# Recalling a compressive memory in transposed layout: one matmul per unit, denominators in a column-tiled pass, reciprocals broadcast by DMA, and projections that begin on two chunks of x

## The chip, the cores and the metric

The kernel runs on one core of a Trainium2 chip. The metric is device time in microseconds (us) of one execution.

Engines are named as in the profile: PE (matmuls; PEld is its weight loads), DVE (the vector engine), ACT (the scalar engine), POOL (GpSimd), SP (the sync engine, which here only issues DMAs; "SPq" in a listing). "L473" is a line of that kernel's own source, so the numbers differ between kernels. A line of a helper (`matmuls`, here L468 or L473) stands for many tiles.

## The reference, cut to what matters

```python
# x: (1, 2048, 512); 32 heads of 16; 4 segments of 512 tokens
g = sigmoid((x * gate_w).sum(-1, keepdims=True))          # one gate per token
for s in range(4):                                        # M, z: memory of the earlier segments
    p = softmax(qs @ ks.T * scale + causal_mask)
    a_dot = p @ vs
    a_mem = (phi(qs) @ M) / ((phi(qs) @ z) + 1e-6)        # the recall, per head
    o = sig(beta) * a_mem + (1 - sig(beta)) * a_dot
    M += phi(ks).T @ vs;  z += phi(ks).sum(tokens)
a = o @ wo
b = ((relu(x @ W_gate)) * (x @ W_up)) @ W_down            # the FFN, F = 1792
return g * a + (1 - g) * b
```

The kernel computes (1 - g) * (r * a + b) with the ratio r = g / (1 - g) = exp(z), so r, one number per token, must reach the attention's outputs.

## The kernel before

A unit is one chunk of 128 channels (eight heads) of one segment; there are 16 units, and 12 of them (segments 1 to 3) recall the memory. A small list scheduler inside the kernel (`plan.add(engine, duration, key, emit, dependencies, latency)`) fixes the order of instructions on every engine before the program is built. A table `SHIFT` of offsets to the keys holds the tuning. Each engine gets its own list in that order and works it in order.

The recall of a unit, with `normalise` shared with the attention itself:

```python
    def recall(seg, c):
        for r in range(2):                                  # even heads, odd heads
            a = plan.add("PE", 216, key + r, lambda r=r, sl=sl: nc.tensor.matmul(
                bank(sl), lhsT=mbd[i][:, c, r].rearrange("p j e -> p (j e)"), rhs=pqT[u % RQ][:],
                start=True, stop=True), ...)
            groups.append((sl, a))
        recalled[u] = normalise(u, 1, key, groups)          # m = 1

    def normalise(u, m, key, groups):
        for r, (sl, a) in enumerate(groups):                # two 128x512 transposes on DVE
            done.append(plan.add("DVE", 633, ..., nc.vector.transpose(T[ts.i][:, r], bank(sl)) ...
        if m: ...  den = den + 1e-6                          # column DH of T
        ...  cfr = reciprocal(den)
        ...  cfr = cfr * grc[i][:, c, m]                     # head gate times r
        ...  och = T[..., 0:DH] * cfr                        # 128x512
    # ... cut
```

The ratio r reaches `grc` through DRAM, from the 128x4 tile `rcol` (token 128t+p in partition p, column t):

```python
            def back():
                for j in range(4):
                    nc.sync.dma_start(out=rq[seg % 2][32 * j:32 * j + 32],
                                      in_=ratio[seg].rearrange("b q t -> q b t"))
            d = plan.add("SP", 360, key, lambda: nc.sync.dma_start(
                out=ratio[seg].rearrange("b q t -> (b q) t"), in_=rcol[:, cols]), [c], 1700)
            d = plan.add("SP", 1440, key, back, [d, ...], 1700)
```

At the start, 10 warm-up matmuls run, then 16 transposes of x (four per chunk), then the projections, each of which needs all four chunks.

The softmax here doesn't subtract the row's maximum and nothing guards it: scores larger than these inputs give would overflow.

Of the kernel before, what the change touches and what calls it, by code (L numbers as in the profile page):

```python
# [7 lines left out]
BF16 = mybir.dt.bfloat16  # L8
F32 = mybir.dt.float32
# [18 lines left out]
RE = 7  # L28
# [4 lines left out]
    21: -90000, 25: -170000, 29: -240000, 31: 210000, 52: 30000, 55: -10000, 58: -140000,  # L33
    74: 40000, 81: 90000, 85: 33000, 87: 80000, 88: -40000, 94: -80000, 115: 80000, 121: 100000,
    145: 130000, 204: -20000, 207: -50000, 210: -20000, 213: -3000, 222: -20000, 227: 270000,
    231: 1500, 234: 15600, 237: 30000, 240: -120000, 243: 11999, 246: 2000, 249: -10000,
    252: -14000, 255: 12999, 261: 28000, 264: -2000, 267: 30000, 270: 15000, 273: 28000,
    276: -10000, 279: 20000, 282: -2000, 300: -120000, 312: 24999, 324: -80000, 339: 80000,
    351: -50000, 354: 60000, 364: -20000, 372: -20000, 377: -50000, 379: 70000, 380: -40000,
    383: -100000, 385: 20000, 398: 10000, 400: 100000, 401: 10000, 404: 16000, 406: -130000,  # L40
    407: -4000, 480: -200000, 481: -190000, 544: 50000, 553: -18000, 556: 6000, 559: -30000,
    562: 2000, 565: -10000, 574: 19000, 583: -20000, 586: -10000, 589: -30000, 592: 9000,
    595: 10000, 598: 27000, 604: 2000, 607: -10000, 610: -4000, 613: -3000, 619: -10000,
    628: 21000, 631: -10000, 637: 29999, 661: 69999, 673: 70000, 686: 180000, 687: 150000,
    688: 100000, 689: -100000, 701: -120000, 704: 140000, 705: 110000, 709: -280000, 714: 15000,
    722: -6000, 727: -60000, 735: 15000, 737: 150000, 748: 8000, 751: -90000, 754: -60000,
    757: -10000, 796: -180000, 800: 90000, 801: 10000, 830: -160000, 831: -20000, 834: 140000,
    869: 30000, 903: 5000, 906: 40000, 909: -3000, 915: -15000, 921: -20000, 924: -10000,
    927: 10000, 930: 30000, 933: 10000, 936: 30000, 942: 30000, 945: -30000, 951: -10000,
    957: -20000, 963: -30000, 969: -20000, 972: 30000, 978: 40000, 984: 24000, 987: 209999,  # L50
    999: 110000, 1011: 60000, 1037: -230000, 1038: 60000, 1039: -260000, 1042: -100000,
    1046: -60000, 1047: 50000, 1052: -40000, 1054: -90000, 1057: 30000, 1062: -80000,
    1067: 56000, 1072: -60000, 1077: -50000, 1082: -70000, 1090: 50000, 1093: -20000,
    1096: 20000, 1134: -30000, 1170: 40000, 1239: 14000, 1242: 90000, 1247: 119999, 1248: 99999,
    1251: 10000, 1254: 60000, 1257: -20000, 1263: -2000, 1266: 20000, 1272: 50000, 1275: 60000,
    1278: 140000, 1284: 50000, 1290: 20000, 1293: -70000, 1296: -30000, 1299: -30000,
    1323: 159999,
# [157 lines left out]
def kernel(  # L215
# [34 lines left out]
    xn = [sb([P, 4, D], BF16, f"xn{i}") for i in range(2)]  # L250
# [17 lines left out]
    mbd = [sb([P, NC, 2, 4, 32], BF16, f"mbd{i}") for i in range(2)]  # L268
    mzacc = sb([P, NC, 2, HW], F32, "mzacc")
    hT = ring([P, L], BF16, "hT", RH)  # L270
    T = ring([P, 2, L], F32, "T", 2)
# [4 lines left out]
    och = ring([P, L], BF16, "och", 4)  # L276
    cfr = ring([P, 2, 16], F32, "cfr", 4)
# [7 lines left out]
    def work():  # L285
# [3 lines left out]
    LANDS = dict(n0=4500, q=5950, k=9300, v=9750, g0=11800, u0=13300, gw=13900, g1=15200, u1=16700,  # L289
                 x1=18400, g2=20400, u2=21600, g3=22800, u3=24000, d0=27700, d1=30400, o=31800, n1=33400,  # L290
                 x2=35200)
# [11 lines left out]
    def load_halves(dst, src, k, name):  # L303
        src = src.rearrange("(c p) n -> p c n", p=P)
        nc.sync.dma_start(out=dst[:, 0:k // 2], in_=src[:, 0:k // 2])
        nc.scalar.dma_start(out=dst[:, k // 2:k], in_=src[:, k // 2:k])
        return arrival(name)
# [4 lines left out]
    def load_xn(seg):  # L312
        nc.sync.dma_start(out=xn[seg % 2][:], in_=x[seg * L:(seg + 1) * L, :].rearrange(
            "(t p) n -> p t n", p=P))
# [12 lines left out]
    got_n[0] = load_halves(xn[0], x[0:L, :], 4, "n0")  # L327
# [9 lines left out]
    got_x[1] = [arrival("x1")]  # L337
# [6 lines left out]
    load_xn(1)  # L344
    got_n[1] = arrival("n1")
    load_xT(2)
    got_x[2] = [arrival("x2")]
    plan.add("SP", 33100, -1e9, None)
# [9 lines left out]
    for j in range(4):  # L358
        nc.vector.memset(mcol_e[32 * j:32 * j + 16, :], 1.0)
    nc.vector.tensor_scalar(mcol_o[:], mcol_e[:], -1.0, 1.0, ALU.mult, ALU.add)  # L360
    bd = sb([P, NC, 8, HW], BF16, "bd")
    nc.gpsimd.memset(bd[:], 1.0)
    nc.gpsimd.affine_select(out=bd[:], in_=bd[:], compare_op=ALU.is_ge, fill=0.0, base=0,
                            pattern=[[0, NC], [-16, 8], [0, HW]], channel_multiplier=1)
    nc.gpsimd.affine_select(out=bd[:], in_=bd[:], compare_op=ALU.is_ge, fill=0.0, base=15,
                            pattern=[[0, NC], [16, 8], [0, HW]], channel_multiplier=-1)
    for i in range(2):
        nc.gpsimd.memset(Vp[i][:, :, :, DH:18], 1.0)
        nc.vector.memset(mbd[i][:], 0.0)
# [13 lines left out]
    gcat = sb([P, NC, 2, 2], F32, "gcat")  # L383
    grc = [sb([P, NC, 2, 2, 16], F32, f"grc{i}") for i in range(2)]
# [4 lines left out]
    ratio = [dram.tile([4, 32, 4], F32, name=f"ratio{i}") for i in range(NSEG)]  # L389
    rq = [sb([P, 4, 4], F32, f"rq{i}") for i in range(2)]  # L390

    def head_gates():
        gb = gcat[:, :, 1, :]
        for j in range(4):
            nc.vector.tensor_copy(ebq[32 * j:32 * j + 32], eb.rearrange(
                "p (c j r) -> p j c r", j=4, r=2)[32 * j:32 * j + 32, j])
        nc.vector.tensor_scalar(gb, ebq[:], 1.0, None, ALU.add)
        nc.vector.reciprocal(gb, gb)
        nc.vector.tensor_tensor(gcat[:, :, 0, :], ebq[:], gb, ALU.mult)
# [3 lines left out]
    got_gates = plan.add("DVE", 1250, 0.0, head_gates, [got_eb], 100, lock=True)  # L403
# [11 lines left out]
    def gate_tasks(seg):  # L415
# [3 lines left out]
        for t in range(4):  # L419
            zs.append(plan.add("DVE", 690, key, lambda t=t: nc.vector.scalar_tensor_tensor(  # L420
                junk[:], xn[seg % 2][:, t, :], 1.0, gwb[:], ALU.mult, ALU.mult,
                accum_out=zc[:, 4 * seg + t:4 * seg + t + 1]), [got_n[seg], got_gw], 60, lock=True))
# [20 lines left out]
        else:  # L443
            src, frees = lambda: rq[seg % 2].rearrange("p b t -> p t b"), []

            def back():
                for j in range(4):
                    nc.sync.dma_start(out=rq[seg % 2][32 * j:32 * j + 32],
                                      in_=ratio[seg].rearrange("b q t -> q b t"))
            d = plan.add("SP", 360, key, lambda: nc.sync.dma_start(  # L450
                out=ratio[seg].rearrange("b q t -> (b q) t"), in_=rcol[:, cols]), [c], 1700)
            d = plan.add("SP", 1440, key, back, [d, att.get(("gate", seg - 2))], 1700)
        war = [att.get(("comb", 4 * seg - 5))]
        att["gate", seg] = plan.add("DVE", 500 if seg else 340, key, lambda: nc.vector.tensor_tensor(
            grc[seg % 2].rearrange("p c m r (t b) -> p (c m r) t b", b=4),
            src()[:, None].to_broadcast([P, 16, 4, 4]),
            gcat.rearrange("p c m r -> p (c m r)")[:, :, None, None].to_broadcast([P, 16, 4, 4]),
# [4 lines left out]
    def matmuls(key, deps, sl, ops, start=True, stop=True, prev=None, width=L, need=()):  # L462
        n = len(ops)
        for k in range(0, n, GM):
# [7 lines left out]
            t = plan.add("PE", 215.8 * width / L * m, key - (0 if first else CONT), emit, deps,  # L472
# [6 lines left out]
    def x0_tasks():  # L479
        done = []  # L480
        for c in range(NC):
            sl = work()

            def pe(c=c, sl=sl):
                tp = bank(sl).bitcast(BF16)
                for t in range(4):
                    nc.tensor.transpose(tp[:, t * P:(t + 1) * P], xn[0][:, t, c * P:(c + 1) * P],
                                        ident[:])
            a = plan.add("PE", 240, K(-9), pe, [got_n[0]], PEL, need=[sl])
            cp = nc.scalar.copy if c % 2 else nc.vector.tensor_copy  # L490
            done.append(plan.add(
                "ACT" if c % 2 else "DVE", 430, K(-9), lambda c=c, sl=sl, cp=cp: cp(  # L492
                    xT[0][:, c, :], bank(sl).bitcast(BF16)[:, 0:L]),
                [a], DVL, frees=[sl]))
        return done
# [14 lines left out]
    def proj_q(seg, c):  # L510
# [4 lines left out]
        a = matmuls(key, got_x[seg] + [got_q] + war, sl, proj_mm(wq_sb, c, seg))  # L515
# [9 lines left out]
    def proj_k(seg, c):  # L525
# [3 lines left out]
        a = matmuls(key, got_x[seg] + [got_k] + war, sl, proj_mm(wk_sb, c, seg))  # L529
# [53 lines left out]
    def attention(seg, c):  # L583
# [47 lines left out]
        a, oc = normalise(u, 0, key, groups)  # L631
        if seg:
            b, om = recalled[u]
            a = plan.add("DVE", 335, key, lambda: nc.vector.tensor_tensor(
                och[oc.i][:], och[oc.i][:], och[om.i][:], ALU.add), [a, b], 110, frees=[om],
                lock=True)
        war = [ffn.get(("o", seg - 2, q)) for q in range(4)]
        att["ot", u] = plan.add("DVE", 633, key, lambda: nc.vector.transpose(
            oT[i][:, c, :], och[oc.i][:]), [a] + war, DVL, frees=[oc])

    recalled = {}

    def normalise(u, m, key, groups):
# [15 lines left out]
        a = done[1]  # L659

        def den():
            return t()[:, :, :, DH]
        if m:
            a = plan.add("DVE", 150, key, lambda: nc.vector.tensor_scalar(
                den(), den(), 1e-6, None, ALU.add), [a], 40, lock=True)
# [176 lines left out]
```

## Time and profile before

| | before |
|---|---|
| time | 278.38 us median of 3 runs (277.8 to 278.51) |
| span of the profiled run | 276.3 us |
| busy: PE / DVE / ACT / POOL | 265.3 / 207.7 / 195.9 / 87.5 us |
| first projection, last matmul (starts) | 7.39, 272.9 us |

Part 1 of the profile's page for the kernel before (busy us, share of the span, instructions):

```profile
PE 265.3 (96%) x2178; PEld 113.1 (41%) x2214; DVE 207.7 (75%) x456; ACT 195.9 (71%) x176; POOL 87.5 (32%) x139
```

PE is the limit, and the span is nearly full of it. Ends of matmuls are modelled, so this share says little about the last few per cent. The rest of this text therefore uses starts: "lag" is what PE has lost, from its first projection up to some matmul, against its own list worked without a wait (0.2158 us per 512 columns, about 0.1 us at each change of the tiling mode, as between 71.93 and 72.03 us; both from the timeline of the kernel before). By that count the kernel before is 7.39 us of start + 260.09 us of PE work + 5.41 us of lag = 272.9 us, the start of the last matmul.

The view of waits, PE's (line, waited for: us in total, times, longest), shows how little is lost to any one cause:

```profile
PE ps L468 <- issue: 1.9, 12, 0.2
PE ps L779 <- DVE mcol_e L357: 1.3, 1, 1.3
PE ps L578 <- ACT E L598: 0.7, 2, 0.4
PE ps L468 <- DVE T L651: 0.6, 2, 0.4
```

The view of windows (start:end, length, then busy us of PE, PEld, DVE, ACT, POOL with the number of instructions, PE's granted clock, DMA share, GB/s) for two stretches:

```profile
60.00:65.00 5.00, 4.75 (x44) 2.04 (x38) 4.56 (x13) 3.30 (x4) 0.64 (x1) 1.00 0.01 3
...
90.00:99.30 9.30, 9.14 (x60) 3.71 (x61) 7.29 (x18) 7.02 (x4) 3.46 (x5) 1.00 0.08 17
```

PE is busy 4.75 of 5 and 9.14 of 9.3 us there, at full clock.

### The profile page before, as it was taken

How to read it: one execution, taken by the hardware profiler on the slowest of the kernel's cores; microseconds unless marked ns; L12 is line 12 of the kernel's file. 1: busy time of each engine (PE TensorE's matmuls, PEld its weight loads, DVE VectorE, ACT ScalarE, POOL GpSimd, SP SyncE). 2: the span in 40 equal slices, each digit the busy share in tenths (PEclk: the TensorE clock that was granted, in tenths of full speed). 3: DMA queues.
4: the chain of work that ended last, by engine and by line, in shares of the span. 5: the costliest groups of instructions: out<-in, count | busy, mean ns of one | idle time of the engine just before them, and what ended most of it. 6: DMA issues, size and time to landing. Idle time of an engine off the chain costs nothing.

```text
span 276.3 us, 5510 instructions
## 1 busy us (share of the span) xinstructions
PE 265.3 (96%) x2178; PEld 113.1 (41%) x2214; DVE 207.7 (75%) x456; ACT 195.9 (71%) x176; POOL 87.5 (32%) x139
## 2 busy tenths in 40 slices
PE   8899999989999999999999999999999999999995
PEld 4343444433343433434343434343444334344543
DVE  3688989999898869698998768999228785638322
ACT  2299898968897778899996878778847776734100
POOL 5013333432424343534334343333301435230000
PEclk9999999999999999999999999999999999999999
DMA  7999965100411100100001000000000000000001
GB/s 233 316 269 347 268 93 171 13 14 0 97 22 20 23 19 21 21 0 19 4 0 36 7 19 5 19 19 2 0 0 4 19 21 19 21 0 0 2 28 48
DMA packets 27993, 15.46 MB, mean 56 GB/s; under 512 B 15680, under 2 KB 27968, under 8 KB 27968
## 3 DMA queue, kind: packets, MB, share of 16 engines
q1 hardware_dynamic: 26752, 14.06, 19.4%
q10 hardware_dynamic: 1216, 1.06, 1.1%
q8 instruction: 17, 0.28, 0.4%
q14 instruction: 8, 0.07, 0.1%
HBM read 9.86 MB, written 2.10 MB: 43 GB/s over the span
## 4 chain that ended last, share of the span: by engine, by line
PE 81%; DVE 10%; ACT 4%; issue 4%; DVEq 0%; ACTq 0%
PE ps L468 63%; PE ps L578 8%; PE ps L620 6%; PE ps L681 2%; ACT E L598 2%; PE ps L779 2%; DVE hT L743 1%; ACT ex L507 1%; DVE ktr L532 1%; DVE T L651 1%; DVE junk L420 1%; DVE QT L517 1%; ACT rgr L737 1%; DVE och L656 1%; ACT Vp L561 0%
## 5 line engine op out<-in xcount | busy, mean ns | idle before, releaser
L598 ACT ACTIVATE E<-ps 128x2048 bf16<-128x2048 f32 x80 | 150.6, 1882 | 31.5 <-PE ps L578 26.8
L607 POOL TENSOR_SCALAR_AFFINE_SELECT E<-E 128x512 bf16<-128x512 bf16 x128 | 83.9, 671 | 157.5 <-ACT E L598 157.5
L743 DVE TENSOR_TENSOR hT<-ps,rgr 128x512 bf16<-128x512 f32 x56 | 38.2, 685 | 29.3 <-PE ps L468 21.4
L468 PE MATMUL ps<-xT,wg_sb 128*128 128x512 bf16 x214 | 56.9, 379 | 1.3 <-issue 0.3
L468 PE MATMUL ps<-xT,wu_sb 128*128 128x512 bf16 x220 | 55.8, 380 | 0.8 <-issue 0.5
L468 PE MATMUL ps<-wd_sb,hT 128*128 128x512 bf16 (+1 forms) x233 | 54.5, 367 | 0.8 <-issue 0.5
L737 ACT ACTIVATE rgr<-ps 128x512 bf16<-128x512 f32 x56 | 32.6, 603 | 16.1 <-PE ps L468 11.5
L651 DVE STREAM_TRANSPOSE T<-ps 128x512 f32<-128x512 f32 x56 | 37.3, 694 | 7.1 <-PE ps L620 5.0
L468 PEld LDWEIGHTS <-hT 128*128 128x128 bf16 x238 | 21.9, 98 | 25.1 <-issue 3.9
L468 PEld LDWEIGHTS <-wg_sb 128*128 128x128 bf16 x224 | 20.6, 98 | 26.5 <-issue 4.8
L468 PEld LDWEIGHTS <-wu_sb 128*128 128x128 bf16 x224 | 20.5, 98 | 26.4 <-issue 4.6
L765 DVE TENSOR_SCALAR osr<-ps,ngcol 128x512 bf16<-128x512 f32 (+1 forms) x17 | 12.1, 709 | 13.9 <-PE ps L468 13.9
L620 PE MATMUL ps<-E,Vp 128*17 128x256 bf16 (+3 forms) x512 | 20.8, 300 | 0.4 <-DVE hT L743 0.4
L507 ACT ACTIVATE ex<-ps 128x512 bf16<-128x512 f32 x24 | 14.4, 599 | 9.6 <-DVE ktr L532 7.1
L656 DVE TENSOR_TENSOR och<-T,cfr 128x512 bf16<-128x512 f32 x28 | 20.6, 736 | 0.4
L578 PE MATMUL ps<-QT,KTe 32*128 32x512 bf16 (+3 forms) x256 | 17.3, 302 | 0.7 <-ACT E L598 0.4
L578 PE MATMUL ps<-QT,KTo 32*128 32x512 bf16 (+3 forms) x256 | 17.1, 299 | 0.5 <-ACT E L598 0.4
L468 PE MATMUL ps<-wv_sb,xT 128*128 128x512 bf16 x62 | 16.7, 380 | 0.6 <-DVE T L651 0.4
L468 PE MATMUL ps<-wo_sb,oT 128*128 128x512 bf16 (+1 forms) x65 | 16.9, 366 | 0.3 <-issue 0.2
L468 PE MATMUL ps<-xT,wk_sb 128*128 128x512 bf16 x57 | 16.6, 380 | 0.4 <-ACT ex L507 0.3
L468 PE MATMUL ps<-xT,wq_sb 128*128 128x512 bf16 x59 | 16.0, 379 | 0.8 <-DVE xT L492 0.4
L620 PEld LDWEIGHTS <-Vp 128*17 128x17 bf16 x512 | 10.9, 91 | 12.9 <-issue 3.9
(70 smaller groups left out, 189.2 us busy)
## 6 DMA issues: line engine op xcount, KB each, us to landing
out_dram<-osr SPq DMA_DIRECT2D x15, 128.0 KB, 1.7
wd_sb<-in_B_W_down_dram SPq DMA_DIRECT2D x2, 896.0 KB, 9.9
xn<-in_A_x_dram SPq DMA_DIRECT2D x3, 512.0 KB, 4.0
wg_sb<-in_B_W_gate_dram SPq DMA_DIRECT2D x2, 512.0 KB, 9.2
wu_sb<-in_B_W_up_dram SPq DMA_DIRECT2D x2, 512.0 KB, 9.4
wg_sb<-in_B_W_gate_dram SPq DMA_DIRECT2D x2, 384.0 KB, 5.1
wu_sb<-in_B_W_up_dram SPq DMA_DIRECT2D x2, 384.0 KB, 6.1
wk_sb<-in_A_wk_dram SPq DMA_DIRECT2D x1, 512.0 KB, 7.5
```

The costliest lines, as they stand in the source:

```text
L468: nc.tensor.matmul(bank(sl)[:, 0:width], lhsT=lhsT, rhs=rhs, start=(start and q == 0), stop=(stop and q == n - 1))
L507: return es, plan.add("ACT", 478, key + 500, lambda: nc.scalar.activation(ex1[es.i][:], bank(sl), ACT.Exp), [a], ACL, need=[es], frees=[sl])
L578: nc.tensor.matmul(ps[:, j * L + off:j * L + off + n], lhsT=kt[32 * j:32 * j + 32, kb * P:(kb + 1) * P], rhs=QT[i][32 * j:32 * j + 32, kb ...
L598: nc.scalar.activation(Ef[:, e0 * L:e1 * L], ps[:, e0 * L:e1 * L], ACT.Exp, scale=SCALE),
L607: nc.gpsimd.affine_select(out=m, in_=m, compare_op=ALU.is_ge, fill=0.0, base=0, pattern=[[0, 4], [1, P]], channel_multiplier=-1)
L620: nc.tensor.matmul(bank(sl)[32 * j:32 * j + HW, kb * P:kb * P + w], lhsT=Vp[i][:, kb, 8 * c + 2 * j + r, 0:HW], rhs=E[(NFILL * u + f) % RE ...
L651: done.append(plan.add("DVE", 633, key - RL, lambda r=r, sl=sl: nc.vector.transpose(T[ts.i][:, r], bank(sl)), [a] + done, 60 if r else 0, ...
L656: nc.vector.tensor_tensor(och[ds.i].rearrange("p (q r e) -> p r q e", r=2, e=DH), t()[:, :, :, 0:DH], cfr[cs.i][:, :, :, None].to_broadcas ...
L681: a = plan.add("PE", 216, key + r, lambda r=r, sl=sl: nc.tensor.matmul(bank(sl), lhsT=mbd[i][:, c, r].rearrange("p j e -> p (j e)"), rhs=p ...
L737: r = plan.add("ACT", 478, key - RL, lambda sl=gsl, rs=rs: nc.scalar.activation(rgr[rs.i][:], bank(sl), ACT.Relu), [g], ACL, frees=[gsl])
L743: nc.vector.tensor_tensor(hT[hs1.i][:], bank(sl), rgr[rs.i][:], ALU.mult)),
L765: b = plan.add("DVE", 95 + 1.12 * w, key - RL, lambda: nc.vector.tensor_scalar(osr[os.i][:, 0:w], bank(sl)[:, 0:w], ngcol[:, tt:tt + 1], N ...
```

## The change

The intent is to relieve PE and DVE. In the transposed layout (channels in partitions, tokens in the free dimension) the head gate is folded into the memory matrix, so one matmul gives both even and odd heads. The denominators of four heads' groups come from small column-tiled matmuls, for two units at once. DVE takes their reciprocals and multiplies them by r, now needed with the token in the free dimension; two DMA hops broadcast each head's row over its 16 channels (`cdr`). One DVE product then evicts and scales the recall. The core of the diff:

```diff
-        for r in range(2): ... two matmuls, normalise(u, 1, key, groups)
+    def dens(seg, half):                       # per segment: two halves of two units
+        def pe():
+            for k, c in enumerate(cs):
+                for t in range(4):
+                    nc.tensor.matmul(bank(sl)[32 * t:32 * t + 32, 0:P],
+                        lhsT=zbd[i][:, c].rearrange("p a h -> p (a h)"),
+                        rhs=pqT[...][:, t * P:(t + 1) * P],
+                        start=(k == 0), stop=(k == 1), tile_position=(0, 32 * t))
+        ...  dn = dens + 1e-6;  dn = reciprocal(dn);  dn = dn * rr[i]          # DVE, 128x128
+        plan.add("SP", ... coefs[n].rearrange("h t p -> t h p") <- dn, 2200)
+    def recall(seg, c):
+        b = plan.add("SP", ... cdr <- coefs[n][8 * k:8 * k + 8] ... .to_broadcast([8, 16, L]), 2600)
+        a = plan.add("PE", 216, ... one matmul, lhsT=mbd[i][:, c])
+        a = plan.add("DVE", 605, ... omr = bank(sl) * cdr)
... the ratio by token (rr), new:
+            a = plan.add("SP", 360, key, lambda: nc.sync.dma_start(
+                out=rtok[seg].rearrange("t p -> p t"), in_=rcol[:, cols]), [c], 1900)
+            att["rr", seg] = plan.add("SP", 360, key, lambda: nc.sync.dma_start(
+                out=rr[seg % 2][:], in_=rtok[seg][:, None].to_broadcast([4, 32, P])), [a, ...], 1900)
... the other ratio path, four reads become one broadcast read:
-            back(): 4 x dma_start(rq[32 * j:...] <- ratio "b q t -> q b t")
+            ratio "q b t -> b q t" <- rcol;   rq <- ratio, .to_broadcast([4, 32, 16])
... the start:
-        for k in range(10):   (warm-up matmuls)      x0: chunk by chunk, all four before a projection
+        for k in range(7):                           x0: transposes of chunks 0 and 1 first; a projection's
+                                                     matmul c waits for chunk c alone
... rings: T 2 -> 1, och 4 -> 2, cfr 4 -> 2, E 7 -> 8; a new SHIFT table
```

## The prediction

> **What bounds it now.** TensorE's stream of matmuls. The page gives PE 96% of a 276.3 us span, but ends are modelled, so I counted starts in the timeline. Two 128x512 matmuls start 0.216 us apart[...]. The program holds 241 us of columns. The row-tiled QK groups (80) and column-tiled PV groups (16) each cost about 0.25 us more ([...]here a QK group of 0.213 us takes 0.33 us, and 0.1 us before it). That fills nearly everything from 7.4 us on. Real holes, those of single missing records (0.22 us) set aside, add to about 4 us, mostly at 12 to 23 and 54 to 77 us (PE waiting for VectorE, ScalarE). VectorE is 75% busy over the span, but 88 to 99% in the windows from 20 to 80 us.
>
> **What the change does.**
> 1. Recall on PE: 24 matmuls become 12: -2.6 us. Denominators: 6 groups of 8 column-tiled 128x128, four at a time, about 0.12 us each, linked into PV groups: +0.8 us. Row groups unchanged. Net -1.8 us, all on the critical engine.
> 2. VectorE: a recall unit's two transposes (2 x 0.69), epsilon 0.24, reciprocal 0.35, gate product 0.22, scaling 0.74 = 2.9 us, twelve times, is 35 us. In place: one scaled eviction (about 0.72) twelve times, and six times 1.4 us (reciprocal of 128 columns about 0.95, from 178, 203 and 345 ns at 4, 8 and 32 columns; two small ops). About -18 us: 208 to 190 busy. This pays only through the holes, and those before 60 us have no recall in them: about -1 us of the 4.
> 3. Start: 7 warm-up matmuls instead of 10 end at about 4.3 us instead of 5.6 (loads of weights 0.43 us apart show the half clock). x's halves land at 4.2 and 4.6 us, wq's at 5.6 and 6.0 (issue plus landing). All 16 transposes still precede the projections, but copies of chunks 0 and 1 run under the transposes of 2 and 3. First projection at about 6.1 instead of 7.39 us: -1.3 us, some work at half clock included. wk lands at 9.3 us, as the 16 q matmuls end.
> 4. DMA: about 35 small transfers more. The DMA share is at most 10% after 90 us; a hop takes about 2.5 us and recall has several us of slack: no cost.
> 5. Tail: same sequence.
>
> **Time.** 278.4 - 1.8 - 1.3 - 1.0 = 274.3 us, 1.5% faster. Range 272.3 to 276.4. Chances: faster by over 2% (under 272.8) 0.15, within 2% 0.84, slower 0.01.
>
> **What would show it.** 12 recall matmuls; first projection near 6.1 us; VectorE near 190 us busy and no longer over 90% at 60 to 80 us, while PE's starts there close up; PE share at 96% or above; PE's waits still name QK's exp and the FFN product; stretch after the last PV unchanged.
>
> **What would make it wrong.** The late recall waits on two DMA hops and blocks a PSUM bank or PE's in-order queue; or one T buffer and two och make transposes wait and PSUM banks free later: to 277. Relief of VectorE removing nearly all 4 us of holes: 271.5. The early start lost again before 60 us, where VectorE and ScalarE are near full: 275.5.

## The result, and the profile after

| | before | after |
|---|---|---|
| time, median | 278.31 us (4 runs) | 294.25 us (292.9 to 297.09, 4 runs) |
| span of the profiled run | 276.3 us | 292.8 us |
| busy: PE / DVE | 265.3 / 207.7 us | 271.5 / 191.9 us |
| start + PE work + lag = last matmul's start | 7.39 + 260.09 + 5.41 = 272.9 | 5.70 + 258.37 + 25.29 = 289.4 |

The ratio of after to before is 1.0589, with a 95% interval from 1.0507 to 1.0672: slower. (A ratio here is the mean time of one kernel's runs over that of the other's of the same rounds, so not quite the ratio of the medians quoted. Executions over 1.5% slower than the fastest of the same kernel are left out of the means.)

The work on PE fell by 1.72 us and the first projection came 1.69 us earlier, both close to the prediction. The lag grew by 19.9 us, which swallows both. The waits of PE after:

```profile
PE ps L636 <- DVE omr L728: 7.6, 1, 7.6
PE ps L473 <- DVE T L668: 3.3, 2, 3.1
PE ps L473 <- DVE osr L815: 1.7, 1, 1.7
```

and the same windows, with the one that follows the second hole:

```profile
60.00:65.00 5.00, 2.60 (x28) 1.09 (x17) 1.17 (x4) 0.90 (x2) 0.63 (x1) 1.00 0.06 5
65.00:73.00 8.00, 7.10 (x39) 2.47 (x39) 6.49 (x19) 6.57 (x6) 2.10 (x3) 0.79 0.04 8
...
90.00:99.30 9.30, 1.73 (x10) 0.51 (x9) 1.73 (x5) 1.88 (x1) 2.17 (x3) 0.84 0.48 80
99.30:107.00 7.70, 7.12 (x47) 2.52 (x47) 5.96 (x17) 1.88 (x1) 0.89 (x1) 0.52 0.09 25
```

Two large holes appear, which together hold 10.7 us of waiting. In the first, DVE is idle from 60.73 to 64.53 us and ACT from 60.55 to 64.65; PE works on until 62.83 us and then stands until 65.90. From 60 to 65 us the busy time of PE, DVE and ACT falls to 2.60, 1.17 and 0.90 of 5 us (before: 4.75, 4.56 and 3.30). Between 90 and 99.3 us PE is busy 1.73 us. After each hole the granted clock is low (0.79, then 0.52). In the records of the clock it stands at one half for 3.41 us from 65.66 and for 10.24 us, three times as long, from 96.38. The window of 3.41 us just before each halving held little PE work or none: PE was busy for 0.58 us from 62.25 to 65.66 us, and not at all from 92.97 to 96.38. In the four runs with 4-byte packets, windows at full clock with 0 to 1.30 us of busy PE were followed by half clock, and windows with 1.77 us or more were not; for the return of the clock see the last point of this text. Half clock also makes the busy time of PE misleading here: 271.5 us is more than before, for less work.

What ended these holes, in DVE's timeline (start, us, engine, line, op, tiles; in brackets idle time before and its releaser):

```profile
64.53 1.31 DVE L668 STREAM_TRANSPOSE T<-ps 128x512 f32<-128x512 f32 x2 [3.80 <-remote]
...
98.59 0.69 DVE L728 TENSOR_TENSOR omr<-ps,cdr 128x512 bf16<-128x512 f32 x1 [7.54 <-DMA cdr<-coefs]
```

"Remote" means that the profile found no releaser in the core. The records of semaphore updates say more: this transpose on DVE, and ACT's exponential at 64.65 us, wait for a count that PE raises. PE's work that raises it ended (as modelled) at 60.37, 61.00, 62.40 and 62.84 us, but all four updates are recorded between 64.51 and 64.69, so up to 4.1 us late. DVE and ACT were waiting for news of finished PE work; why it came so late is taken up at the run `rtok_act`. The second hole is a chain of DMAs. The timeline of SP's issues:

```profile
53.85 0.69 SPq L448 DMA_DIRECT2D ratio<-rcol  x1
54.59 0.42 SPq L453 DMA_DIRECT2D rtok<-rcol  x1
60.05 0.56 SPq L450 DMA_DIRECT2D rq<-ratio  x1
64.30 0.52 SPq L455 DMA_DIRECT2D rr<-rtok  x1
...
79.60 0.57 SPq L448 DMA_DIRECT2D ratio<-rcol  x1
80.22 0.47 SPq L453 DMA_DIRECT2D rtok<-rcol  x1
81.57 0.53 SPq L450 DMA_DIRECT2D rq<-ratio  x1
89.57 0.51 SPq L455 DMA_DIRECT2D rr<-rtok  x1
90.18 0.54 SPq L712 DMA_DIRECT2D coefs<-dnr  x1
94.29 1.21 SPq L720 DMA_DIRECT2D cdr<-coefs  x2
```

Read it together with when each DMA's last semaphore update came (from the trace's records of updates; "landing" is that minus the issue):

| DMA | plan assumed | before | after |
|---|---|---|---|
| `rtok<-rcol` (512 packets of 4 B) | 1.9 us | none | 9.69, 9.29, 11.4 us |
| `rq<-ratio`, issued after it | 1.7 | 1.7 to 3.8 | 4.9, 8.1, 8.7 |
| first `coefs<-dnr` | 2.2 | none | 4.1 |
| `cdr<-coefs` (two per half) | 2.6 | none | 3.5 to 4.2, the second of a pair 4.5 to 5.8 |

The store by token issued at 80.22 landed at 89.5. SP works in order, so the read `rr` waited for it and issued at 89.57, and the first coefficients behind it at 90.18, though their reciprocals had been ready at about 83. The coefficients landed at 94.27, the broadcast at about 98.5, and the product `omr` ran at 98.59. It stood first in DVE's list, so everything else stood too. The issue to landing of the store is four to six times what the plan (and I) had assumed.

### The profile page after: what moved, and what is told of

It reads as the page before. It is cut to its first block, busy times and chain, and to the rows that moved or that the text cites. A ratio compares the mean times of both kernels' runs of the same rounds, so it can differ in the third digit from the quotient of the medians.

```text
span 292.8 us, 5598 instructions
## 1 busy us (share of the span) xinstructions
PE 271.5 (93%) x2247; PEld 112.7 (39%) x2247; DVE 191.9 (66%) x420; ACT 196.7 (67%) x175; POOL 84.6 (29%) x141
## 4 chain that ended last, share of the span: by engine, by line
PE 66%; DMA 12%; DVE 10%; ACT 8%; issue 2%; another core or an unknown queue 1%; POOL 0%; SPq 0%; ACTq 0%; DVEq 0%
PE ps L473 54%; PE ps L594 6%; ACT E L614 4%; PE ps L636 4%; DMA cdr<-coefs 3%; DMA out_dram<-osr 3%; DMA rq<-ratio 3%; DMA coefs<-dnr 2%; ACT ex L521 2%; DVE ktr L548 2%; DVE hT L793 1%; PE ps L829 1%; DVE junk L422 1%; ACT rgr L787 1%
## 5 line engine op out<-in xcount | busy, mean ns | idle before, releaser
L623 POOL TENSOR_SCALAR_AFFINE_SELECT E<-E 128x512 bf16<-128x512 bf16 x128 | 82.5, 662 | 176.8 <-ACT E L614 174.3
L473 PE MATMUL ps<-xT,wu_sb 128*128 128x512 bf16 x224 | 59.8, 386 | 5.7 <-DVE T L668 3.3
L473 PE MATMUL ps<-xT,wg_sb 128*128 128x512 bf16 x224 | 58.5, 380 | 1.1 <-DVE hT L793 1.0
L473 PE MATMUL ps<-wd_sb,hT 128*128 128x512 bf16 (+1 forms) x238 | 56.4, 376 | 0.0
L636 PE MATMUL ps<-E,Vp 128*17 128x256 bf16 (+3 forms) x512 | 22.7, 310 | 8.4 <-DVE omr L728 7.6
L668 DVE STREAM_TRANSPOSE T<-ps 128x512 f32<-128x512 f32 x32 | 21.0, 689 | 8.9 <-PE ps L636 4.9
L728 DVE TENSOR_TENSOR omr<-ps,cdr 128x512 bf16<-128x512 f32 x12 | 8.3, 690 | 17.2 <-DMA cdr<-coefs 14.2
L473 PE MATMUL ps<-xT,wk_sb 128*128 128x512 bf16 x64 | 17.6, 379 | 0.3 <-DVE ktr L548 0.2
```

The lines of the kernel that those rows point to most:

```text
L473: nc.tensor.matmul(bank(sl)[:, 0:width], lhsT=lhsT, rhs=rhs, start=(start and q == 0), stop=(stop and q == n - 1))
L623: nc.gpsimd.affine_select(out=m, in_=m, compare_op=ALU.is_ge, fill=0.0, base=0, pattern=[[0, 4], [1, P]], channel_multiplier=-1)
L636: nc.tensor.matmul(bank(sl)[32 * j:32 * j + HW, kb * P:kb * P + w], lhsT=Vp[i][:, kb, 8 * c + 2 * j + r, 0:HW], rhs=E[(NFILL * u + f) % RE ...
L668: done.append(plan.add("DVE", 633, key - RL, lambda r=r, sl=sl: nc.vector.transpose(T[ts.i][:, r], bank(sl)), [a] + done, 60 if r else 0, ...
L728: a = plan.add("DVE", 605, key - RL, lambda: nc.vector.tensor_tensor(omr[om.i][:], bank(sl), cdr[cs.i][:], ALU.mult), [a, b], DVL, need=[o ...
```

## The experiments

Theory A: the store of the ratio by token, 512 packets of 4 B, and what waits behind it, is the whole of the loss. Rivals: DMA hops in general, of which the change has more (B); the single `T` buffer and the `och` ring of two (C); the two extra issues and the broadcast read in SP's in-order list, whatever their packets (D). Later letters stand for theories about the start, the queue and the orders; the expectations spell them out.

Each experiment is the changed kernel with the edit shown, unless it says otherwise. Times are medians; the kernel before measured 278.4 to 278.8 us beside them.

### The changed kernel again

No edit. This asks whether the holes belong to the program.

> The changed kernel once more, for a second profile. If its two large holes in TensorE's stream (3.2 us before 65.9 us, 7.6 us before 99.3 us) belong to the program, both stand here again within half a microsecond, with the clock halved after each, at 292 to 297 us. If the first was an accident of one profiled execution, it is gone here and the time stays.

Measured: 293.01 us, span 291.0, clock 0.977. Both holes stand again at the same places: DVE is idle from 60.71 to 64.51 us, and PE waits for `omr`:

```profile
PE ps L636 <- DVE omr L728: 6.7, 2, 6.5
```

The second hole is 6.5 us long, 1.1 us shorter than the first time, so outside the half microsecond expected. Half clock follows again (3.41 us from 66.86, 10.24 us from 94.17). The holes are the program's; their exact lengths are not. (A single run; its state is unknown.)

### The store and read of the ratio by token taken away

```diff
-            out=rtok[seg].rearrange("t p -> p t"), in_=rcol[:, cols]), [c], 1900)      # store
-            out=rr[seg % 2][:], in_=rtok[seg][:, None].to_broadcast(...)), [...], 1900)   # read
+            (both tasks stay in the plan, nothing is issued);  rr = 1.0 once, at the start
```

This is wrong: r is replaced by 1 in the recall. (With these inputs r is near 1, so the comparison does not notice.)

> Wrong result on purpose: the store of the ratio by token and its read back are not issued, and the denominators are multiplied by ones; everything else and all orders stay. Theory A: both large holes go (the one before 66 us too, if the 512 small writes hold up what else runs on these rings), the clock stays at full after 5 us, and the time is 274 to 279 us. Theories B and C: 288 us or more.

Measured: 278.03 us (276.82 to 279.23), ratio 0.9985 (0.9949 to 1.002); span 276.4, clock 1.0. The windows again:

```profile
60.00:65.00 5.00, 4.61 (x90) 2.21 (x78) 4.19 (x14) 4.45 (x5) 1.27 (x2) 1.00 0.01 3
...
90.00:99.30 9.30, 9.06 (x60) 3.73 (x61) 7.19 (x20) 7.26 (x6) 3.12 (x5) 1.00 0.08 22
```

Both holes are gone, with all other hops (`ratio`, `rq`, `coefs`, `cdr`), the single `T` buffer and the two `och` still in place. The rivals "DMA hops in general" and "one T and two och" fall. All 16 us by which the changed kernel lies above the one before hang on this pair of DMAs. But 278.0 is also not the predicted 274.3; that is taken up below.

### Order on the sync engine alone

```diff
-                out=rtok[seg].rearrange("t p -> p t"), in_=rcol[:, cols]), [c], 1900)
+                out=rtok[seg].rearrange("t p -> p t"), in_=rcol[:, cols]), [c], 10000)
```

The scheduler is told of the late landing. The orders of PE, DVE, ACT and POOL stay the same; on SP, only segment 2's read `rr` moves behind the first coefficients and their broadcast.

> One number of the kernel's own scheduler is changed: the landing time that it assumes for the four-byte store of the ratio by token, 1.9 us, becomes 10. The order on PE, DVE, ACT and POOL stays as it was; on the DMA queue alone the read of segment 2's ratio goes behind the first coefficients. Theory A (head of the queue: the first coefficients stand behind a read that waits 9 us for that store): the hole before 99 us shrinks from 7.6 to under 2 us, its half clock goes, and the time falls by 9 to 12 us to 282 to 285; the hole before 66 us stays. Theory B (two hops through DRAM are too slow in themselves) and theory C (one T buffer and two och hold VectorE up): the hole stays at 5 us or more and the time at 290 or more.

Measured: 289.96 us (288.95 to 292.17; a fourth, 294.62, was slow and is left out), ratio 1.0428; the expectation of 282 to 285 was missed.

```profile
80.03 0.47 SPq L453 DMA_DIRECT2D rtok<-rcol  x1
...
82.75 0.55 SPq L712 DMA_DIRECT2D coefs<-dnr  x1
91.66 1.22 SPq L720 DMA_DIRECT2D cdr<-coefs  x2
```

```profile
PE ps L636 <- DVE omr L728: 4.6, 1, 4.6
```

The coefficients now issue at 82.75, right when they are ready, yet land 8.89 us later, 2 us after the store (89.46): what was issued behind the store still completes behind it, though no longer in SP's list. By the packet records it was not waiting to begin: the 128 packets of `coefs` begin between 83.93 and 87.79 us. The store is alike: the one issued at 54.59 us in the changed kernel has begun all its packets by 55.91 and lands at 64.28. So packets begin soon, and their completion is what comes late. The hole shrinks only from 7.6 to 4.6 us. So the in-order list accounts for some 2 to 3 us of the second hole (3.0 of the 7.6 us, 1.9 of the 6.5 us in `again`), and reordering does not cure the cause.

### The same store with other packets

```diff
-                out=rtok[seg].rearrange("t p -> p t"), in_=rcol[:, cols]), [c], 1900)
+                out=rtok[seg].rearrange("t (q b) -> (t q) b", b=4), in_=rcol[:, cols]), [c], 1900)
```

The same 2 KB and the same issue, but 128 packets of 16 B. Tokens land in wrong places.

> The changed kernel with one edit: the store of the ratio by token writes its 512 values as 128 contiguous packets of 16 B instead of 512 packets of 4 B. The tokens land in wrong places (wrong on purpose; the ratio is near 1 for these inputs, so the comparison may still pass). Same issues, same two hops, same broadcast read, order of every engine unchanged. Theory A (the 512 small packets are the cost): the store lands about 2 to 2.5 us after its issue, as the other ratio store of 128 packets of 16 B did (2.0 to 2.4 us) instead of 9 to 11; both large holes go; 278.0 to 279.5 us. Rival D (two more issues in the in-order queue of the sync engine, or the broadcast read of 64 KB, cost as much): holes of 3 us or more stay before 66 and 99 us; 284 us or more.

Measured: 278.25 us (277.23 to 279.35), ratio 0.9993 (0.9963 to 1.0023); the output is wrong, by 0.021. The store lands 2.27, 2.46 and 1.53 us after its issue. The windows, and its place among SP's issues:

```profile
60.00:65.00 5.00, 4.60 (x52) 2.06 (x44) 4.22 (x12) 4.45 (x5) 1.27 (x2) 1.00 0.02 3
90.00:99.30 9.30, 9.14 (x61) 3.72 (x61) 7.56 (x20) 7.30 (x6) 3.44 (x5) 1.00 0.07 17
```

```profile
54.14 0.69 SPq L448 DMA_DIRECT2D ratio<-rcol  x1
54.89 0.45 SPq L453 DMA_DIRECT2D rtok<-rcol  x1
56.23 0.56 SPq L450 DMA_DIRECT2D rq<-ratio  x1
57.18 0.52 SPq L455 DMA_DIRECT2D rr<-rtok  x1
```

Compare the lines at 54.59 and 64.30 of the changed kernel: the read follows its store by 2.3 us here and by 9.7 us there. The holes are gone with two issues, two hops and the 64 KB read all kept. So theory A holds and rival D falls: it is the form of the store, 512 packets of 4 B. The edit changes the size of the packets, their number and their scatter (4 B pieces, 512 B apart in DRAM) together, so which of the three does the harm is not separated.

### The small packets on another queue

```diff
-            a = plan.add("SP", 360, key, lambda: nc.sync.dma_start(
+            a = plan.add("ACT", 60, key, lambda: nc.scalar.dma_start(
                 out=rtok[seg].rearrange("t p -> p t"), in_=rcol[:, cols]), [c], 1900)
```

> The changed kernel with one edit: the store of 512 packets of 4 B is issued from the scalar engine's queue instead of the sync engine's. Orders of the tensor, vector, scalar and gpsimd engines unchanged but for these three issues; on the sync engine the first store of coefficients now stands one place earlier, ahead of the read of the ratio by token. Theory G (the store harms what shares its queue): it may still land late, but the other ratio's hop, the coefficients and the outputs land in their usual 2 to 2.7 us, the quiet stretch at 60 to 64 us goes, and the time is 278 to 283 us. Rival H (the store harms whatever runs on the same transfer engines, from any queue): the other ratio's hop still lands 5 us or later, the quiet stretch at 60 to 64 us stays, and the time is 288 to 294 us.

Measured: 287.0 us (286.71 and 287.29, two runs only), ratio 1.0294; clock 0.986. The store lands after 9.04, 8.09 and 7.55 us, and the other ratio's store, issued at the same moment from SP, after 9.21, 7.39 and 7.25 (without the small packets: 2.0 to 2.4). Windows and waits:

```profile
60.00:65.00 5.00, 3.23 (x59) 1.52 (x48) 2.64 (x11) 2.41 (x2) 0.63 (x1) 1.00 0.04 4
...
90.00:99.30 9.30, 5.59 (x44) 2.13 (x45) 6.67 (x18) 2.35 (x2) 1.53 (x2) 0.67 0.45 73
```

```profile
PE ps L636 <- DVE omr L728: 3.0, 1, 3.0
PE ps L473 <- DVE T L668: 1.8, 2, 1.6
```

The quiet stretch stays, shortened (PE busy 3.23 of 5 us), and ends at 63.4 us, when the store lands. Theory G (only its own queue suffers) falls. Rival H holds in its mechanism; its time, 288 to 294 us, was a little too high, probably since the first coefficients now issue ahead of the read `rr`. So the damage is not bound to the queue; it lies in something that the queues share. Whether that is the transfer engines or the memory behind them, these runs do not separate.

How one DMA can quiet several engines at once is shown in part. DVE and ACT lacked neither input nor, as far as the records show, instructions: they waited for PE's updates of its semaphore, and these came late (see the result). The same four updates are late in all four runs with 4-byte packets, and the first of them comes within 0.25 us of the landing of the store: at 64.51 us (store 64.28) in the changed kernel, 64.49 (64.44) in `again`, 64.44 (64.49) in `rr_later`, 63.41 (63.36) here. In the kernel before and in the runs `no_rtok`, `rtok16` and `tr_rtok` no update by PE was more than 0.3 us late. A packet suffers too: the 16 KB packet of the instruction queue that begins at about 61 us takes 3.70, 3.44, 4.09 and 2.99 us in those four runs, and 0.94 to 1.35 us in the others. The stretch cannot have waited for this packet in two of the four runs, where it ended later than the stretch (65.05 us in `rr_later`, 64.16 here). So updates by PE and completions of other DMAs both come late while this store is unfinished; why, stays open.

### A ratio by token without DMA

```diff
-   rtok store, rr read;   ratio store, rq read
+   ratio spread over 32 columns (DVE, 128x4x32), one f32 matmul with the identity, copy to rr;
+   the gate's columns through the fold matmul, as segment 0 does it already
```

> A repair: the ratio by token and the gate's columns of segments 1 to 3 are made by two small matmuls each instead of four DMAs through DRAM; the coefficients still go out and back by DMA. The result stays right. Theory A: no hole over 2 us, clock at full throughout, 273 to 278 us, so level with or ahead of the kernel before. Theories B and C: the hole before the first coefficients stays at 5 us or more and the time at 286 or more.

Measured: 282.96 us (282.61 to 283.02), ratio 1.0158, correct; the expectation of 273 to 278 was missed. There is no large hole; the clock is 1.0. But the PE work is 1.25 us more, and the lag 12.5 us, in many small waits:

```profile
PE ps L600 <- ACT E L620: 2.8, 7, 0.7
...
PE ps L479 <- ACT rgr L793: 0.7, 1, 0.7
PE ps L479 <- DVE hT L799: 0.6, 1, 0.6
```

New tasks had moved the numbers by which the `SHIFT` table addresses tasks, so the tuning probably no longer fitted. So this run shows that the holes go with the DMA also when r is right. Its lag is 12.5 us, instead of 8.7 without the store; that the tuning is the reason was not tested, and the run does not measure the idea.

### The early start, undone

```diff
-        for k in range(7):        # the kernel without the store by token
+        for k in range(10):
```

> The kernel without the store by token (278.0 us), with 10 warm-up matmuls instead of 7: the first projection starts about 1.2 us later (5.9 to about 7.1 us), everything else in the same order. The prediction counted an earlier start in full. Theory E (the earlier start is given back within 40 us because PE there waits for ScalarE and VectorE): 277.6 to 278.5 us, and the lag that PE gathers by 40 us falls from 3.2 to about 2 us. Rival F (the start counts in full and the lag by 40 us is the price of the new order alone): about 279.2 us.

Measured: 277.5 us (277.27 to 277.83), ratio 0.9967 (0.9955 to 0.998). The first projection starts at 6.85 instead of 5.92 us, and the last matmul at 272.4 instead of 273.0. Starting 0.9 us later costs nothing. By 40 us, however, the lag is 2.75 us, not the 2 expected: about half of the delay is made up by then, the rest later. And the time is 0.1 us below the range.

### The early start, given to the kernel before

```diff
-        for k in range(10):       # the kernel before
+        for k in range(7):
```

> The kernel before, with 7 warm-up matmuls instead of 10 and nothing else: transposes of x can begin when x lands (4.5 us) instead of 5.5 us; first projection about 6.4 instead of 7.4 us. If the earlier start counts in full (rival F): about 277.3 us. If it is given back (theory E): 278.0 to 278.6 us.

Measured: 278.44 us (278.09 to 278.65), ratio 0.9999 (0.9986 to 1.0011). The first projection starts at 6.44 instead of 7.39 us, 0.95 us earlier, and the lag by 40 us is 2.22 instead of 0.95 us, 1.27 us more: the gain is used up before 40 us. One line of PE's waits is new:

```profile
PE ps L468 <- DMA wk_sb<-in_A_wk_dram: 0.7, 1, 0.7
```

wk lands at about the same time (9.46 us, and 9.28 in the kernel before) however early PE is ready for it. In both kernels an earlier start is worth nothing, as theory E has it. That it is given back by 40 us holds here, and for about half of it in `late`. The waits named are those for weights, ScalarE and VectorE, which are not earlier.

### A correct store in larger packets

```diff
+            e = Task("DVE", 90, key, lambda: nc.vector.transpose(rT[:], rcol[:]), [c], DVL, lock=True)
+            e.n = len(plan.tasks) - 0.5;  extra.append(e)          # keeps the other tasks' numbers
+            def store():
+                for b in range(4):
+                    nc.sync.dma_start(out=rtok[seg][:, 32 * b:32 * b + 32],
+                                      in_=rT[32 * b + 4 * seg:32 * b + 4 * seg + 4])
-            a = plan.add("SP", 360, key, ... out=rtok[seg].rearrange("t p -> p t"), in_=rcol[:, cols], [c], 1900)
+            a = plan.add("SP", 1440, key, store, [e], 1900)
```

A transpose of 32x32 blocks on DVE brings 32 tokens into one row, so four stores of four packets of 128 B replace 512 packets of 4 B (`rcol` is widened to 32 columns, and nulled once). The orders of the engines stay as they were, but for one group of four matmuls near 60 us and the copies that follow it.

> A correct kernel: the changed one, but VectorE first transposes the ratios in 32x32 blocks, so that the store by token has 16 packets of 128 B (in four issues) instead of 512 of 4 B. One small VectorE operation and three issues more per segment; orders of all engines all but unchanged (one group of matmuls moves by two places). Theory A: the store lands in about 2 us after the last issue, no large hole, 278.0 to 279.5 us, a tie with the kernel before, and the clock granted stays 1.0. Rival D: four issues more in the same queue make the holes larger: over 290 us.

Measured: 276.68 us (276.28 to 277.68), correct, ratio 0.9942 (0.9922 to 0.9962): 0.6% faster than before, which is the same by the 2% line, and 17 us faster than the change as it stood.

```profile
60.00:65.00 5.00, 4.61 (x82) 2.18 (x74) 4.91 (x15) 4.45 (x5) 1.28 (x2) 1.00 0.06 16
...
90.00:99.30 9.30, 9.14 (x61) 3.73 (x61) 7.76 (x21) 7.30 (x6) 3.49 (x5) 1.00 0.07 17
```

Each store lands 1.14 to 1.6 us after its issue, or 2.2 to 2.6 where four of them meet other transfers. The expectation was 278.0 to 279.5; against the run without the store, 1.4 us of lag between 200 and 210 us is missing (0.38 instead of 1.76), where PE had waited 1.01 us for DVE's `hT` and 0.56 for `omr`. The orders there are the same in both programs. The second `cdr` of that place landed 4.15 us after its issue here, 5.06 there; why it did is open.

### New orders, for both kernels

The run without the store (278.0) and the correct one (276.7) still lie above the predicted 274.3 us. Two delays stood in the traces that the kernel's scheduler does not know of. First, from the page of the changed kernel (without the store: 10.2 and 8.4 us in place of 9.8 and 8.0):

```profile
L521 ACT ACTIVATE ex<-ps 128x512 bf16<-128x512 f32 x24 | 14.1, 599 | 9.8 <-DVE ktr L548 8.0
```

Second, from the waits for `cdr` in the run without the store:

```profile
  DMA cdr<-coefs: 7.8, 7
```

The exponential of a projection sat idle 9.8 us, 8.0 of them put down to DVE's copy `ktr` out of the same PSUM bank. The plan lets both read the bank at once. The traces show no such case: of the 24 exponentials in the kernel before and the 24 in the changed one, none overlaps DVE's copy (`ktr` or `QT`) out of its bank (the banks are read from the two programs as built). In 16 and 13 of them the copy came first (in the timeline of the kernel before, `ex` starts at 12.20 us, 0.03 us after `ktr` ends), in the others the exponential did, and the later of the two began at least 0.03 us after the end of the earlier. What holds it back is not shown. And `omr` waits for the broadcast, which lands later than the planned 2.6 us even without the small packets (the second `cdr` near 205 us after 5.06 us).

```diff
-    def phi_exp(key, sl, a):             ... ACT.Exp ..., [a]
+    def phi_exp(key, sl, a, cp):         ... ACT.Exp ..., [a, cp]      # cp: the copy by DVE
-    cdr: 2600        ratio, rq: 1700     rtok, rr: 1900      coefs: 2200
+    cdr: 4100 / 5000 ratio, rq: 2300     rtok, rr: 2600      coefs: 2500
     SHIFT = { ... }                      # searched anew by random local changes
```

The scheduler was told the one order, copy first. The search ran offline on the scheduler's model, which served to find orders, not to tell times. `retuned` is the correct kernel with the 128-byte packets and new orders; `retuned_before` is the kernel before with the one delay that concerns it and new orders, from a search of about the same length.

> The correct kernel with the store in 128-byte packets, its orders searched anew after telling its own scheduler three things that the traces show and it did not know: [...]the broadcast of coefficients lands after 4.1 us (first of a pair) and 5.0 us (second) instead of 2.6; the other small hops land after 2.3 to 2.6 us instead of 1.7 to 2.2. Theory J (what kept the kernel without the store at 278.0 instead of the predicted 274.3 us is lag from orders found under wrong delays): lag falls from 8.7 to 4 or 5 us, 272.5 to 275.0 us. Rival K (the lag is the price of the longer recall chain, whatever the order): 276 to 278 us.

> The kernel before, its orders searched anew in the same way and for as long, with the one delay that concerns it (the exponential waits for the copy). It tells what of the retuned kernel's gain belongs to the change. Theory L (the change itself is worth its 1.7 us of matmuls and some 1 to 1.5 us of vector work, once both are tuned alike): 275 to 277.5 us here, 2 to 4 us above the retuned changed kernel. Rival M (tuning alone makes the gain): within 1 us of the retuned changed kernel.

Measured: `retuned` 272.45 us (271.82 to 273.22), correct, ratio 0.9782 (0.9758 to 0.9806); `retuned_before` 274.36 us (274.23 to 274.5), correct, ratio 0.9842 (0.9819 to 0.9865).

| start + PE work + lag | first 20 us of lag | rest of the lag |
|---|---|---|
| before: 7.39 + 260.09 + 5.41 = 272.9 | 0.1 | 5.3 |
| without the store: 5.92 + 258.37 + 8.73 = 273.0 | 1.5 | 7.2 |
| `retuned`: 5.38 + 258.14 + 3.19 = 266.7 | 1.5 | 1.7 |
| `retuned_before`: 7.47 + 260.19 + 1.74 = 269.4 | 0.0 | 1.7 |

PE's waits in `retuned` are down to one during the warm-up (the first line; the kernel before has it too), weights that have not landed yet, and trifles:

```profile
PE ps L968 <- DVE mcol_e L482: 1.3, 1, 1.3
PE ps L612 <- DMA wk_sb<-in_A_wk_dram: 0.6, 1, 0.6
PE ps L612 <- DMA wv_sb<-in_A_wv_dram: 0.5, 1, 0.5
PE ps L612 <- DVE T L807: 0.3, 1, 0.3
```

```profile
PE 264.2 (98%) x2247; PEld 111.0 (41%) x2247; DVE 191.9 (71%) x423; ACT 195.3 (72%) x175; POOL 84.2 (31%) x142
```

Theory K falls, and theory J holds in its outcome: the lag was a matter of orders. It fell to 3.2 us, below the 4 to 5 expected, and the time is a hair below its range. That the wrong delays were the reason is not shown: the delays were corrected and the search run anew in one step, and a new search with the old delays was not tried. `retuned` beats the kernel before by 2.2% (interval 1.9 to 2.4, so unclear at the 2% line). But most of that is tuning: `retuned_before` gets 1.6% without any of the change, below the 275 to 277.5 us of theory L. Tuned alike, the change is worth 274.36 - 272.45 = 1.9 us, just under the 2 to 4 us of theory L and clearly over the 1 us of theory M. The two ledgers say from where: 2.05 us less PE work, 2.1 us of earlier start, 1.5 us of which is lost by 20 us (0.6 and 0.5 us of it to the weights in the listing); the rest of the lag is the same, 1.7 us, though DVE works 191.9 us in one and 207.7 in the other. (The spans of the two profiled runs are 2.7 us apart, somewhat more than the medians.) So once the orders fit, relief of DVE buys nothing by this count.

## Why the prediction was wrong, point by point

The prediction, 274.3 us with 272.3 to 276.4, was wrong: 294.25 us, and slower, which had been given a chance of 0.01.

- **Step 4, "DMA: ... a hop takes about 2.5 us and recall has several us of slack: no cost." This is the step that failed.** It took the duration of the hops that the trace showed (1.7 to 3.8 us) for a new hop of another form. The store by token is 512 packets of 4 B, and it landed after 9.3 to 11.4 us. Without it, 278.03 us; with the same store in packets of 16 B, 278.25: the three such stores (one per segment from the second) cost 16 us. Part of this is work that waited for it directly (SP's in-order list, then `coefs`, `cdr`, `omr`, PV), part is other transfers that it delayed from about 2 to between 5 and 9 us, part is the quiet stretch near 60 us, where PE's own updates came up to 4.1 us late, and part is half clock for 13.7 us after the two holes. The slack of "several us" was not enough for a chain of hops behind it.
- **"What would make it wrong" named the waits on DMA hops, and sized them at most to 277.** Right in kind, far off in size.
- **Step 1, PE work -1.8 us.** It fell by 1.72 us. Right.
- **Step 2, DVE from 208 to 190 us, worth about -1 us of holes.** DVE: 191.9 us, right. Between 40 and 80 us the lag grew by 2.64 us before and by 0.66 us without the store, so 2.0 us came back there, more than counted (that DVE's relief is the cause fits, but was not tested by itself). After 80 us it was given back: the lag grew by 1.82 us before and by 4.88 us without the store, part of it in waits that the recall's own chain brought (PE for `omr`, 0.56 us at 205 us, while `cdr` landed later than planned; 1.01 us for `hT` at 208). Tuned alike, the rest of the lag is the same with and without the relief.
- **Step 3, the start, -1.3 us.** The first projection came 1.7 us earlier, as the mechanism said. The term's worth is what failed: the lag by 40 us was 3.2 us without the store and 0.95 before. Delaying the start again by 0.9 us cost nothing (277.5), and giving it to the kernel before brought nothing (278.44). The prediction had named this risk ("the early start lost again before 60 us") and counted the gain in full all the same.
- **Step 5, the tail.** From the last matmul's start to the end, 3.4 us before and 3.5 us after. Right.

Without the store the sum is -1.5 (start) - 1.7 (PE work) + 2.2 (lag to 40 us) - 2.0 (40 to 80 us) + 3.1 (after 80 us) = +0.1 us for the last matmul, and 278.0 us is what was measured. Of what should have shown each step, the recall's 12 matmuls, DVE near 190 us and the unchanged tail came true; "PE's waits still name QK's exp and the FFN product" did not: they name `omr` and `T`. Nor did "PE share at 96% or above": it was 93% in the changed kernel.

What stays open: why PE's semaphore updates and the completions of other DMAs come late while such a store is unfinished, whether the size, the number or the scatter of its packets matters, and what share of the 16 us falls to each of the paths above; they were only removed together.

## What to carry to other kernels

When a transposed store turns partitions into the fast dimension, count its packets and their bytes before anything else: three stores of 512 packets of 4 B cost 16 us here, while a 32x32 block transpose on the vector engine and packets of 128 B carried the same numbers for nothing. Do not price a new DMA by the landing of an old one of another shape, and do not count an earlier start before looking at what the next stage waits for (here weights that land when they land). When a tuned order meets changed work, tune both kernels again with the delays that the trace shows before judging the change: here tuning was worth 4.1 us to the old kernel, and the change 1.9 us on top.

## What the runs measured of small stores and of the clock

- The same 2 KB by token, from issue to landing: 128 packets of 16 B took 1.5 to 2.5 us (`rtok16`), 16 packets of 128 B in four issues 1.1 to 2.6 us (`tr_rtok`), 512 packets of 4 B 7.6 to 11.4 us (all four runs with it).
- The harm crosses queues (`rtok_act`): another small store issued from SP took 7.3 to 9.2 us beside a store of 4-byte packets issued from ACT, 2.0 to 2.4 us without it.
- Compute engines go quiet beside such a store: in the four runs with it DVE stood still for 2.3 to 3.8 us, ACT for 2.6 to 4.1 and PE for 1.6 to 3.1, PE's semaphore updates came up to 4.1 us late, and a 16 KB packet of the instruction queue took 3.0 to 4.1 us instead of 0.9 to 1.4.
- The first `cdr` of the changed kernel, whose slowest dimension is 8, shows nine semaphore updates: one at 95.30 us, about 1.0 us after its issue begins, and eight from 97.67 to 98.50 us. Such a transfer, 256 KB to 128 partitions, took 3.4 to 4.9 us over all runs, and 4.2 to 5.8 us for the second of a pair.
- At half clock in the changed kernel's records, PE's weight loads come 0.43 us apart (103.25 to 106.24 us); at full clock 128x512 matmuls start 0.216 us apart. In the kernel before, the records of full clock begin at 6.43 us; up to then the warm-up's loads are 0.43 us apart and the transposes of x 0.107, after it 0.056. After the second hole of the changed kernel (PE resumed at 99.33 us) the window from 99.79 to 103.20 us, in which PE was busy 2.86 of 3.41 us, mostly with row- and column-tiled matmuls, was followed by another at half clock; full clock returned at 106.62 us. In `rr_later` full clock followed a window with 2.83 of 3.41 us busy (96.07 to 99.48 us), in the repeat `again` one with 3.08 (101.00 to 104.41 us). So the busy time that the profile counts does not decide it, and what does is not shown.
